# Adding the attention mask with VectorE as the scores leave PSUM, instead of with two TensorE products

## The chip, the cores and the metric

One NeuronCore of one Trainium2 chip runs the whole program; nothing is shared with another core. A NeuronCore has five engines with a queue each: TensorE (PE; matrix products into PSUM, with its weight loads shown apart as PEld), VectorE (DVE), ScalarE (ACT), GpSimd (POOL) and SyncE (SP), which here only issues DMAs. The metric is device microseconds of one execution, the median of several; lower is better.

## The reference, cut to what matters

Four sequences of 576 tokens go through masked attention with 8 heads of 64 columns, then through a gated layer (2304 tokens, 512 to 1536 to 512) and a soft mixture of 8 experts. The change concerns the attention:

```python
scores = scale * np.matmul(q, k.transpose(0, 1, 3, 2))
rel = pos[:, None] - pos[None, :]
mask_plain = (rel >= 0) & (rel < window)                                   # heads 0 to 3, window 32
mask_dil = (rel >= 0) & (rel < window * dilation) & (rel % dilation == 0)  # heads 4 to 7, dilation 4
scores = np.where(masks[None], scores, -1000000000.0)
scores = scores - np.max(scores, axis=-1, keepdims=True)
attn = np.exp(scores)
attn = attn / (np.sum(attn, axis=-1, keepdims=True) + 1e-09)
return np.matmul(attn, v)
```

A query sees at most 32 keys, which lie in a window of 64 keys for each group of 32 queries; the kernel computes the scores of these windows alone.

## The kernel before, in words

**Units.** The attention is cut into 20 units: five blocks of tokens (blocks 0 to 3 have 512 tokens, block 4 the 256 that remain) by four pairs of heads. A unit has the scores of two heads (`r`), each as a PSUM tile of 128 partitions by 4 x 64 columns, `s_ps[r]`, in the first half of a PSUM bank. `scores` (L140) fills it: first a product of a 128x128 identity with a mask tile (three masks of 256 columns in bf16, zero or a large negative number, in `msk`), which starts the accumulation (L148, once for each `r`), then 32 small products for each, 64 keys by 32 queries, that add the scores (L162). `softmax` (L172) takes on VectorE the maximum of each row and 64 columns, straight from PSUM (L176, once for each `r`), and subtracts it, from PSUM into the tile `s` in SBUF (L178, once for each `r`); then ScalarE takes the exponential in place (L184, 128x512), VectorE sums it (L186), adds 1e-9 (L187) and takes the reciprocal (L188), and VectorE (block 0) or GpSimd (later blocks) multiplies (L189). `turn_unit` transposes the result (L195, L196), `weighted` multiplies with v (L222), `finish_unit` splits the output into a high and a low part (L250 on ScalarE, L251 on VectorE) or copies it (L237, L238). From block 1 on, the output of the unit before the last is written into the second half of the same two banks (`beside["bank"]`), so two units share a bank: scores of the younger and output of the older one.

**Stages.** The head of the program (to about 28 us) works through the 4 units of block 0, with loads that were issued in a written order. Then layer 1 of block 0 runs on TensorE (`l1`, L455: 24 groups of 12 products 128x512, two groups for each of 12 column blocks), while 5 steps of later units and the conversion of the weights from a packed form (`convert`, L367: L379 on ScalarE, L380 and L381 on VectorE, L382 on GpSimd; split into high and low parts by `split_w`, L433 and L434) are placed between the groups. Layer 1 of block 1 follows with the rest of the units, to about 215 us; a `Spread` object decides after which group a step comes. After that: blocks 2 and 3 as a pair, block 4, the experts. Each group of layer 1 ends in a PSUM tile of a ring of two, which ScalarE's sigmoid (L477) or VectorE's multiplication (L479) empties.

**Order.** A planner places the instructions in the engines' queues when the program is built, by priorities and costs of its own; an engine works its queue in that order. Instructions marked by `keep_in_program_order` hold their written order among themselves: from layer 1 on, the score products, transposes and products with v are so marked (`at`, L137). Sigmoid and multiplication have a raised priority (L475). Waits are set by the framework; it lets two engines touch a PSUM bank only one after the other.

Of the kernel before, what the change touches and what calls it, by code (L numbers as in the profile page):

```python
# [13 lines left out]
ALU = mybir.AluOpType  # L14
AX = mybir.AxisListType
PSUM = bass.MemoryType.PSUM

P = 128
# [17 lines left out]
M_ID, M_COLS = 768, 896  # L36
# [9 lines left out]
def k_window(n, hp, t, i):  # L46
    if n < 4:
        return 32 * (4 * t + i) if hp < 2 else 160 * i + 32 * t
    return 160 * t + 32 * i if hp < 2 else 64 * (4 * t + i)
# [7 lines left out]
def tile_kernel(  # L57
# [10 lines left out]
    nc = tc.nc  # L68
# [17 lines left out]
    msk = cpool.tile([P, M_COLS], BF16, name="msk")  # L86
    cst = cpool.tile([P, C_COLS], F32, name="cst")
    mask = msk[:, 0:M_ID].rearrange("p (m c) -> p m c", m=3)
# [48 lines left out]
    def at(ins):  # L137
        return tc.keep_in_program_order(ins) if grouped[0] else ins

    def scores(u, ts):  # L140
        n, hp = u["id"]
        q, k = u["qk"][:, 0:512], u["qk"][:, 512:1536]
        if "s_ps" not in u:
            u["bank"] = [ps_a.tile([P, 512], F32, tag="a", name=f"s_ps{r}") for r in range(2)]
            u["s_ps"] = [x[:, 0:256].rearrange("p (t c) -> p t c", t=4) for x in u["bank"]]
            for r in range(2):
                at(
                    nc.tensor.matmul(  # L148
                        u["s_ps"][r].rearrange("p t c -> p (t c)"),
                        lhsT=msk[:, M_ID:M_COLS],  # L150
                        rhs=mask[:, 2 if n == 4 else (1 if hp >= 2 else 0)],
                        start=True,
                        stop=False,
                        skip_group_check=True,
                    )
                )
        for t in ts:
            for i in range(4):
                for r in range(2):
                    o = k_window(n, hp, t, i)  # L160
                    at(
                        nc.tensor.matmul(  # L162
                            u["s_ps"][r][32 * i : 32 * i + 32, t, :],
                            lhsT=q[64 * r : 64 * r + 64, 128 * t + 32 * i : 128 * t + 32 * i + 32],
                            rhs=k[64 * r : 64 * r + 64, o : o + 64],
                            start=False,
                            stop=True,
                            skip_group_check=True,
                        )
                    )  # L170

    def softmax(u, norm):  # L172
        s = u["s"].rearrange("p (a c) -> p a c", a=8)
        mx = sm.tile([P, 8], F32, tag="mx", name="mx")
        for r in range(2):
            nc.vector.tensor_reduce(mx[:, 4 * r : 4 * r + 4], u["s_ps"][r], AX.X, ALU.max)  # L176
        for r in range(2):
            nc.vector.tensor_tensor(  # L178
                s[:, 4 * r : 4 * r + 4],
                u["s_ps"][r],  # L180
                mx[:, 4 * r : 4 * r + 4].unsqueeze(2).to_broadcast([P, 4, 64]),
                ALU.subtract,
            )
        nc.scalar.activation(s, s, AF.Exp, scale=0.125)  # L184
        su = sm.tile([P, 8], F32, tag="su", name="su")
        nc.vector.tensor_reduce(su, s, AX.X, ALU.add)  # L186
        nc.vector.tensor_scalar(su, su, 1e-9, None, ALU.add)  # L187
        nc.vector.reciprocal(su, su)  # L188
        norm.tensor_tensor(s, s, su.unsqueeze(2).to_broadcast([P, 8, 64]), ALU.mult)  # L189
# [69 lines left out]
    def attn_steps(pbs, norm, head=None):  # L259
# [30 lines left out]
        def s_step(z, ts=range(4)):  # L290
            if z == 0 and 0 in ts:
                if head:
                    load_qk(0)
                    ld(nc.sync.dma_start(msk, masks.bitcast(BF16)))
                    load_qk(1)
                    ld(nc.sync.dma_start(cst, consts))
                    load_v(0)
                    load_qk(2)
                    load_v(1)
                    head()  # L300
                    load_qk(3)
                    load_v(2)
                    load_v(3)
                else:
                    first(load_qk)
                    first(load_v)
            scores(us[z], ts)
            if 3 not in ts:
                return
            if 2 <= z and not head:  # L310
                weighted(us[z - 2], range(2), us[z])
            softmax(us[z], norm)
            load(z + 2, load_qk)
            if z == 0:
                load(2, load_v)
# [703 lines left out]
    for f in range(NF):  # L1019
        c = f % 4  # L1020
# [18 lines left out]
    for e in range(8):  # L1039
        for h in range(2):  # L1040
            for kc in range(ND):
                nc.tensor.matmul(  # L1042
                    h_ps[h][32 * kc : 32 * kc + 32],
                    lhsT=st[:, kc, 32 * e : 32 * e + 32],
                    rhs=ew[0, e, h][:, kc],
                    start=(e == 0),
                    stop=(e == 7),
# [228 lines left out]
```

## Time and profile before

| | |
|---|---|
| time, median of 3 runs | 507.33 us (505.53 to 507.93) |
| span of the profiled execution, first to last instruction | 502.6 us (no other time of this execution is given) |
| instructions | 12872 |
| TensorE busy | 471.9 us, 94% of the span |
| VectorE busy | 312.1 us, 62% |
| ScalarE busy | 269.8 us, 54% |
| GpSimd busy | 158.1 us, 31% |
| DMA, largest queue | 111.06 MB, 59.2% of 16 engines |

The span is the profile's own time base: all positions below are microseconds from its start. An engine's busy share is a mean over stages that differ; the rows further down show stretches. In the profile's rows `L162` is line 162 of the kernel, "x64" a number of instructions, and a bracket `[0.58 <-ACT x_hi L250]` the time that the engine was idle before the row and what ended that idle time. A row with several instructions gives the time from the first start to the last end.

### The profile page before, as it was taken

How to read it: one execution, taken by the hardware profiler on the slowest of the kernel's cores; microseconds unless marked ns; L12 is line 12 of the kernel's file. 1: busy time of each engine (PE TensorE's matmuls, PEld its weight loads, DVE VectorE, ACT ScalarE, POOL GpSimd, SP SyncE). 2: the span in 40 equal slices, each digit the busy share in tenths (PEclk: the TensorE clock that was granted, in tenths of full speed). 3: DMA queues.
4: the chain of work that ended last, by engine and by line, in shares of the span. 5: the costliest groups of instructions: out<-in, count | busy, mean ns of one | idle time of the engine just before them, and what ended most of it. 6: DMA issues, size and time to landing. Idle time of an engine off the chain costs nothing.

```text
span 502.6 us, 12872 instructions
## 1 busy us (share of the span) xinstructions
PE 471.9 (94%) x5488; PEld 359.1 (71%) x5488; DVE 312.1 (62%) x629; ACT 269.8 (54%) x458; POOL 158.1 (31%) x132
## 2 busy tenths in 40 slices
PE   6889999899999998999789999999999999999993
PEld 3568877688787886786547888888888879842552
DVE  3978888748685755445967665665546765532632
ACT  2569657657697656544856455455436654300223
POOL 0244545415463514126045233333321124200100
PEclk9789999999999999999999999999999999999998
DMA  8979967985998059320002202202399986578997
GB/s 321 409 251 355 345 229 268 326 292 183 355 310 337 4 172 399 128 85 1 2 0 85 83 1 83 85 0 84 97 366 418 370 316 243 209 270 347 425 410 261
DMA packets 23786, 112.15 MB, mean 223 GB/s; under 512 B 2352, under 2 KB 7216, under 8 KB 14640
## 3 DMA queue, kind: packets, MB, share of 16 engines
q1 hardware_dynamic: 23408, 111.06, 59.2%
q8 instruction: 43, 0.70, 0.6%
q10 hardware_dynamic: 320, 0.26, 0.2%
q14 instruction: 15, 0.12, 0.1%
HBM read 97.16 MB, written 14.16 MB: 221 GB/s over the span
## 4 chain that ended last, share of the span: by engine, by line
PE 68%; DVE 6%; ACT 6%; DMA 2%; issue 2%; POOL 1%; SPq 0%; DVEq 0%; ACTq 0%; POOLq 0%
PE l1ps L467 23%; PE pa L589 11%; PE pe L589 6%; PE tp L754 4%; PE so_ps L1101 3%; PE lt_ps L718 3%; PE h_ps L1042 3%; PE pd L589 2%; PE s_ps L222 2%; PE sp L783 2%; DMA wo<-fw 2%; PE s_ps L162 2%; PE op L1140 1%; PE tr L195 1%; DVE s L553 1%
## 5 line engine op out<-in xcount | busy, mean ns | idle before, releaser
L467 PE MATMUL l1ps<-x_hi,whl 128*128 128x512 f32 x384 | 131.3, 407 | 5.7 <-ACT g L477 3.0
L467 PEld LDWEIGHTS l1ps<-x_hi,whl 128*128 128x128 f32 x384 | 72.2, 189 | 23.9 <-ACT g L477 4.2
L467 PE MATMUL l1ps<-x_lo,whl 128*128 128x512 f32 x192 | 76.3, 397 | 0.0
L382 POOL TENSOR_TENSOR fw<-fw 128x512 int32<-128x512 int32 x36 | 49.6, 1387 | 58.8 <-DVE fw L381 24.7
L479 DVE TENSOR_TENSOR g<-l1ps,g 128x512 f32<-128x512 f32 (+1 forms) x36 | 21.6, 599 | 32.4 <-PE l1ps L467 27.7
L467 PEld LDWEIGHTS l1ps<-x_lo,whl 128*128 128x128 f32 x192 | 36.6, 190 | 6.6 <-DVE x_lo L251 0.2
L467 PE MATMUL l1ps<-x,whl 128*128 128x256 f32 x288 | 37.3, 286 | 0.0
L467 PEld LDWEIGHTS l1ps<-x,whl 128*128 128x128 f32 x288 | 35.5, 192 | 0.6 <-ACT g L477 0.2
L434 POOL TENSOR_TENSOR whl<-w,whl 128x512 fp32r<-128x512 f32 x12 | 15.9, 1330 | 51.7 <-ACT whl L433 35.6
L477 ACT ACTIVATE g<-l1ps 128x512 f32<-128x512 f32 (+1 forms) x36 | 19.0, 527 | 22.4 <-PE l1ps L467 22.2
L754 PE MATMUL tp<-cst,g 128*128 128x128 f32 x216 | 27.9, 275 | 0.0
L754 PEld LDWEIGHTS tp<-cst,g 128*128 128x128 f32 x216 | 23.9, 140 | 5.1 <-issue 3.3
L759 ACT COPY gt<-tp 128x512 f32<-128x512 f32 x27 | 15.5, 583 | 21.2 <-PE tp L754 18.4
L379 ACT ACTIVATE fw<-st 128x512 f32<-128x512 f32 x36 | 22.7, 673 | 6.5 <-DMA st<-wd 6.3
L477 ACT ACT_TABLE_LOAD x20 | 25.7, 1283 | 0.4
L380 DVE TENSOR_SCALAR fw<-fw 128x512 uint32<-128x512 uint32 x36 | 23.5, 664 | 2.2 <-ACT fw L379 1.1
L434 POOL TENSOR_TENSOR whl<-wst,whl 128x512 fp32r<-128x512 f32 x12 | 16.3, 1357 | 25.1 <-ACT whl L433 17.9
L652 DVE TENSOR_TENSOR tm<-pe,tm 128x512 f32<-128x512 f32 x12 | 8.3, 690 | 23.7 <-PE pe L589 23.7
L176 DVE TENSOR_REDUCE mx<-s_ps 128x4 f32<-128x256 f32 x40 | 15.3, 414 | 11.1 <-PE s_ps L162 7.9
L189 POOL TENSOR_TENSOR sm<-sm,su 128x512 f32<-128x512 f32 x12 | 14.1, 1172 | 25.4 <-DVE su L188 25.4
L184 ACT ACT_TABLE_LOAD x16 | 20.5, 1283 | 1.0 <-PEq L1266 0.7
L434 DVE TENSOR_TENSOR whl<-fw,whl 128x512 fp32r<-128x512 f32 x24 | 19.1, 811 | 2.9 <-ACT whl L433 2.5
(462 smaller groups left out, 1006.9 us busy)
## 6 DMA issues: line engine op xcount, KB each, us to landing
ew<-w SPq DMA_DIRECT2D x32, 1024.0 KB, 8.7
st<-wd SPq DMA_DIRECT2D x18, 1024.0 KB, 9.1
wst<-wg SPq DMA_DIRECT2D x12, 1024.0 KB, 7.7
v<-qkv SPq DMA_DIRECT2D x20, 512.0 KB, 6.3
wg<-fw SPq DMA_DIRECT2D x12, 512.0 KB, 7.0
w<-wg SPq DMA_DIRECT2D x6, 1024.0 KB, 7.0
qk<-qkv SPq DMA_DIRECT2D x10, 576.0 KB, 6.0
qk<-qkv SPq DMA_DIRECT2D x8, 528.0 KB, 5.4
```

Source lines behind the costliest of these rows:

```text
L176: nc.vector.tensor_reduce(mx[:, 4 * r : 4 * r + 4], u["s_ps"][r], AX.X, ALU.max)
L184: nc.scalar.activation(s, s, AF.Exp, scale=0.125)
L379: nc.scalar.activation(top, st[:, c, 1].bitcast(F32), AF.Prelu, scale=2.0**-112, alpha=2.0**32)
L380: nc.vector.tensor_scalar(top.bitcast(U32), top.bitcast(U32), 3, None, ALU.logical_shift_left)
L382: nc.gpsimd.tensor_tensor(low.bitcast(I32), top.bitcast(I32), low.bitcast(I32), ALU.add)
L434: (nc.gpsimd if pool[h] else nc.vector).tensor_tensor(whl[:, 1, h], src[:, h], whl[:, 0, h].bitcast(F32), ALU.subtract)
L467: nc.tensor.matmul(pt[:, 0:nt], lhsT=whl[:, w_, a, dc, :], rhs=x_[n][:, dc, :], start=first, stop=(dc == HP_ORDER[-1] and w_ == 1),)
L477: nc.scalar.activation(g, pt[:, 0:nt], AF.Sigmoid)
L479: nc.vector.tensor_tensor(g, pt[:, 0:nt], g, ALU.mult)
L589: nc.tensor.matmul(pt, lhsT=w[:, w_, P * c : P * c + P], rhs=x_[:, c], start=first and c == 0 and w_ == 0 and x_ is hi, stop=c == 1 and w_ ...
L754: nc.tensor.transpose(tp[:, c], g_sb[self.n, 4 * q + c][:, P * j : P * j + P], ident)
L759: nc.scalar.copy(to, tp)
```

## The change

The two products of the identity and the mask go; the score products start their own accumulation. In `softmax` VectorE adds the mask to each of the two PSUM tiles and writes the sums into `s` in SBUF; the maximum and the subtraction then each take the whole 128x512 tile in SBUF in one instruction. The exponential and what follows stay.

```diff
@@ scores
-            for r in range(2):
-                at(
-                    nc.tensor.matmul(
-                        u["s_ps"][r].rearrange("p t c -> p (t c)"),
-                        lhsT=msk[:, M_ID:M_COLS],
-                        rhs=mask[:, 2 if n == 4 else (1 if hp >= 2 else 0)],
-                        start=True,
-                        stop=False,
-                        skip_group_check=True,
-                    )
-                )
...
-                            start=False,
+                            start=True,
                             stop=True,
@@ softmax
+        n, hp = u["id"]
+        m = mask[:, 2 if n == 4 else (1 if hp >= 2 else 0)].rearrange("p (t c) -> p t c", t=4)
         for r in range(2):
-            nc.vector.tensor_reduce(mx[:, 4 * r : 4 * r + 4], u["s_ps"][r], AX.X, ALU.max)
-        for r in range(2):
-            nc.vector.tensor_tensor(
-                s[:, 4 * r : 4 * r + 4],
-                u["s_ps"][r],
-                mx[:, 4 * r : 4 * r + 4].unsqueeze(2).to_broadcast([P, 4, 64]),
-                ALU.subtract,
-            )
+            nc.vector.tensor_tensor(s[:, 4 * r : 4 * r + 4], u["s_ps"][r], m, ALU.add)
+        nc.vector.tensor_reduce(mx, s, AX.X, ALU.max)
+        nc.vector.tensor_tensor(s, s, mx.unsqueeze(2).to_broadcast([P, 8, 64]), ALU.subtract)
         nc.scalar.activation(s, s, AF.Exp, scale=0.125)
```

## Rows read from the trace of the kernel before

**Rows 1.** Stretch; busy us (instructions) of PE, PEld, DVE, ACT, POOL; clock; DMA.

```profile
16.00:28.00 12.00, 10.18 (x211) 7.81 (x212) 11.23 (x24) 6.55 (x14) 4.31 (x3) 0.72 0.99 390
28.00:100.00 72.00, 67.28 (x898) 52.94 (x897) 58.79 (x116) 51.67 (x81) 34.00 (x27) 1.00 0.83 295
100.00:215.00 115.00, 112.35 (x1957) 89.12 (x1956) 70.91 (x156) 77.45 (x123) 45.06 (x36) 1.00 0.66 239
```

**Rows 2.** The same for L148 alone: PE and PEld busy, clock, DMA.

```profile
0.00:28.00 28.00, 1.80 (x8) 0.72 (x8) 0.82 0.94 362
28.00:100.00 72.00, 1.96 (x10) 0.58 (x10) 1.00 0.83 295
100.00:215.00 115.00, 4.29 (x22) 1.51 (x22) 1.00 0.66 239
```

**Rows 3.** TensorE's waits, 28 to 215 us: total, times, longest.

```profile
PE l1ps L467 <- ACT g L477: 3.0, 3, 1.7
...
```

**Rows 4.** Chain that ended last, in order of time: start, us, what.

```profile
100.72 0.23 PE s_ps L148 x2
```

**Rows 5.** Timeline of TensorE: start, us, instruction.

```profile
100.33 0.39 PE L467 MATMUL l1ps<-x_hi,whl 128*128 128x512 f32 x1
100.56 0.39 PE L148 MATMUL s_ps<-msk 128*128 128x256 bf16 x2
100.88 0.86 PE L162 MATMUL s_ps<-qk 64*32 64x64 f32 x64
```

**Rows 6.** VectorE's groups by form: busy us, mean ns | idle before.

```profile
L434 DVE TENSOR_TENSOR whl<-fw,whl 128x512 fp32r<-128x512 f32 x24 | 19.1, 811 | 2.9 <-ACT whl L433 2.5
...
L176 DVE TENSOR_REDUCE mx<-s_ps 128x4 f32<-128x256 f32 x40 | 15.3, 414 | 11.1 <-PE s_ps L162 7.9 <-PE s_ps L222 3.1
...
L178 DVE TENSOR_TENSOR sm<-s_ps,mx 128x256 f32<-128x256 f32 x32 | 11.9, 408 | 0.0
L186 DVE TENSOR_REDUCE su<-sm 128x8 f32<-128x512 f32 x16 | 10.9, 682 | 7.6 <-ACT sm L184 7.3
...
L189 DVE TENSOR_TENSOR sm<-sm,su 128x512 f32<-128x512 f32 x4 | 2.7, 680 | 0.0
```

**Rows 7.** Timeline of VectorE, 88.5 to 95.5 us.

```profile
89.54 0.74 DVE L176 TENSOR_REDUCE mx<-s_ps 128x4 f32<-128x256 f32 x2
90.21 0.74 DVE L178 TENSOR_TENSOR sm<-s_ps,mx 128x256 f32<-128x256 f32 x2
```

**Rows 8.** Timeline of ScalarE, the same stretch.

```profile
90.70 0.37 ACT L250 CAST x_hi<-s_ps 128x256 fp32r<-128x256 f32 x1 [3.16 <-DVE sm L178]
91.09 1.28 ACT L184 ACT_TABLE_LOAD   x1
92.39 0.63 ACT L184 ACTIVATE sm<-sm 128x512 f32<-128x512 f32 x1
...
94.33 0.60 ACT L477 ACTIVATE g<-l1ps 128x512 f32<-128x512 f32 x1
```

**Rows 9.** Timeline of ScalarE, 113 to 117 us.

```profile
113.50 1.28 ACT L184 ACT_TABLE_LOAD   x1
116.23 0.63 ACT L184 ACTIVATE sm<-sm 128x512 f32<-128x512 f32 x1 [1.45 <-DVE sm L178]
```

**Rows 10.** Timeline of GpSimd, 88.5 to 95.5 us.

```profile
89.70 1.29 POOL L382 TENSOR_TENSOR fw<-fw 128x512 int32<-128x512 int32 x1 [0.36 <-DVE fw L380]
```

**Rows 11.** Timeline of VectorE in the head.

```profile
12.33 0.42 DVE L176 TENSOR_REDUCE mx<-s_ps 128x4 f32<-128x256 f32 x1 [1.50 <-PE s_ps L162]
...
24.60 0.75 DVE L251 TENSOR_TENSOR x_lo<-xp,x_hi 128x256 fp32r<-128x256 f32 x2 [0.58 <-ACT x_hi L250]
```

**Rows 12.** Timeline of TensorE in the head.

```profile
11.13 1.18 PE L162 MATMUL s_ps<-qk 64*32 64x64 f32 x64 [2.44 <-DMA qk<-qkv]
```

**Rows 13.** The chain again, 181 to 192 us.

```profile
181.41 0.61 ACT g L477
...
182.35 8.59 DMA wo<-fw
```

## The prediction

> **What bounds the kernel now.** I read the busy time by stretch first. The 20 attention units run before 215 us, and the change touches nothing else. From 28 to 100 us TensorE is busy 67.28 of 72 us, from 100 to 215 us 112.35 of 115; VectorE has 58.79 and 70.91 there [rows 1]. So TensorE lacks 7.4 us in all, VectorE 57.3, of which only 13.2 lie ahead of 100 us. Before 28 us it is different: from 16 to 28 us VectorE is busy 11.23 of 12 us and TensorE 10.18, at a granted clock of 0.72. The removed products, looked up by their line, are 8 before 28 us, 10 up to 100 us and 22 after it [rows 2]: 4, 5 and 11 units. What TensorE waited for from 28 to 215 us is read next: the largest item is 3.0 us in three waits on ScalarE's sigmoid [rows 3]. The chain of waits runs through the products themselves: 0.23 us for the two of a unit [rows 4]. So 16 units stand in a stretch where TensorE sets the pace, and 4 in a head that DMA, VectorE and latency set.
>
> **TensorE: what goes.** Per unit two products 128x256 in bf16 leave. The chain gives the pair 0.23 us. From the start of the pair to the first score product 0.32 us pass (100.56 to 100.88), against 0.23 us from one layer-1 product to the next (100.33 to 100.56) [rows 5]; the 0.1 us by which 0.32 exceeds the chain's row may be what the switch to the small score products costs, and then it stays. I take 0.23, with 0.32 as the upper end and, as lower end, nothing where TensorE would have to wait anyway. 16 units x 0.23 = 3.7 us (0 to 5.1). The other score products only get another start flag: same count, same shape, nothing.
>
> **VectorE: what comes.** Before, a unit has two maxima 128x256 from PSUM (414 ns) and two subtractions 128x256 from PSUM (408): 1.64 us. After, two additions, one maximum and one subtraction over 128x512 in SBUF. The addition is not in the trace; nearest is the subtraction from the same PSUM tile, 408 ns; its second operand is a bf16 tile in SBUF, and I take the same figure (ends: 0.34, half of what 128x512 in SBUF took, and 0.49, 408 by the ratio of 811 to 680 below). The maximum has a twin, the sum over 128x512 in SBUF, 682 ns. The subtraction has a twin in the head's normalisation, 128x512 with a broadcast operand, all in SBUF, 680 ns; the low parts of the weights, also two SBUF operands, took 811 ns on average [rows 6]. Sum 0.82 + 0.68 + 0.68 = 2.18 us, so +0.54 us per unit (+0.4 to +0.8 by these ends). From 100 us on, 11 x 0.54 = 5.9 us lie in 44 us of idle VectorE; from 28 to 100 us, 5 x 0.54 = 2.7 us in 13.2. I cost both at nothing; with the cover gone they cost 5.9 and 2.7, at the upper end 8.8 and 4.0.
>
> **The path to the sigmoid.** What matters more than VectorE's sum is what ScalarE waits for. At 89.54 us VectorE starts the maxima, at 90.21 the subtractions [rows 7]. ScalarE, idle 3.16 us until the first subtraction is over, then evacuates the older unit's output from the same bank (90.70), loads a table (91.09), takes the exponential (92.39), and after another load the sigmoid (94.33) [rows 8], which TensorE awaits (the 1.7 us of rows 3). So the bank holds the evacuation, and that holds table load and exponential: 2.85 us from the first maximum to the exponential. The load does not itself wait for the scores: at 113.50 one ran, and the exponential then stood idle 1.45 us for the subtraction [rows 9]. After the change the first bank is read once. The evacuation may start after one addition (0.41 us), and with it and the load (0.37 + 1.28) the exponential could start some 2.1 us after the first addition; VectorE's 1.41 us (89.54 to 90.95) become about 1.95. So the exponential comes some 0.7 us earlier where this order holds, in two of the three waits. Up to -1.3 us; below, nothing, or +0.54 at each of three where the evacuation is planned behind the exponential (+1.6). I take -0.6: one of the two.
>
> One term stands against it. The maxima and subtractions kept their 0.74 us a pair while GpSimd ran an addition in SBUF from 89.70 to 90.99 [rows 7, 10], and their large operand lies in PSUM. The new subtraction has both operands in SBUF, like the weights' low parts, whose mean is 131 ns above the 680 of the head [rows 6]. GpSimd is busy 79 of the 187 us [rows 1], so a subtraction meets it in 42% of cases and may be held for up to one such addition (1.29 us). Worked out as half of it at 42%, that is 0.27 us a unit; it stays inside VectorE's idle time, except in the rival below.
>
> [...]
>
> **The head.** Units 0 and 1 get +1.1 us of VectorE time, but VectorE then stands idle 1.50 us until the scores of unit 2, which wait 2.44 us for their q and k from HBM [rows 11, 12]; hidden. The first scores no longer stand behind the mask's transfer and products (0.3 us at most): hidden by the same transfer. The 0.54 us of unit 2 lie ahead of the first weight conversion in VectorE's queue, and so of the first block's layer 1; those of unit 3 ahead of a spot where VectorE is idle 0.58 us [rows 11]. I take +0.5 us, one unit's; ends 0 and +2.4 (two units, each subtraction held 0.65). Eight products fewer also leave TensorE idle a little longer in a stretch at clock 0.82 [rows 2]; scores took 1.18 us after the idle stretch at 11.13 us [rows 12], and 0.86 in the other units, so up to 0.3 us for each of two units; I take nothing.
>
> **Sum.** -3.7 - 0.6 + 0.5 = -3.8 us on a span of 502.6. After 215 us everything hangs on TensorE's order and moves along. The span is 4.7 us under the median of 507.33 (the page gives no other time of that execution); I keep this distance: 503.5 us. The likeliest case alone: 501.5 to 506.
>
> **Rivals.**
> *VectorE becomes the bound before 100 us (slower).* It is 94% busy from 16 to 28 us and 82% from 28 to 100 [rows 1]; a conversion chain (VectorE, GpSimd, ScalarE, VectorE) feeds layer 1 there. If the 7 units from unit 2 on put their whole increase on the path, with the hold at GpSimd, that is 7 x (0.54 + 0.27 to 0.65) = 5.7 to 8.3 us, less the 3.7 from TensorE: +2.0 to +4.6, some 510.5. It decides from the point where the increase exceeds VectorE's idle time between two layer-1 groups that need a converted weight. Against it: 13.2 us idle for 5 units. For it: rows 3 show waits on the sigmoid that end in a busy VectorE.
> *The gain is given back (same).* The chain goes through a transfer of 8.59 us at 182.35, which starts after the sigmoid of 181.41 [rows 13]. Were it bound to the DMA queue and not to that sigmoid, the 14 units ahead of it would win nothing (14 x 0.23 = 3.2 us); with the head's 0.5 us, 507. A planner that orders the engines' queues anew from its own costs can also take 2 to 3 us: the waits of rows 3 are that large.
> *More is gained.* The pair is worth 0.32, and both waits on the sigmoid shrink: -5.1 - 1.3 + 0.5 = -5.9, 501.5.
> That the products stay cannot be: nothing else writes the mask.
>
> **Chances.** Forecast 0.45, more gained 0.13, given back 0.23, VectorE bound 0.19. A change of 0.5% (2.5 us, under 504.8 or over 509.9) is about what a measurement can tell. Of the forecast's 0.45 some 0.32 lies under 504.8; with 0.13 of the larger gain, 0.45 faster. The rest of the forecast (0.13), the given-back case (0.2) and a small part of the VectorE case (0.04) make 0.37 the same; 0.18 slower. Range 500.5 to 510: it reaches into the slower case, and leaves out its far end and that of the large gain.
>
> **What would show it.** No product of the mask's line; layer-1 product to first score product in 0.23 to 0.33 us; TensorE's busy time from 28 to 215 us down by about 3.7 us, and the stretch shorter by as much. Additions at 0.41 us, the maximum at 0.68, the subtraction at 0.68 alone and near 1.3 where GpSimd runs. ScalarE's evacuation starting behind the first addition. Wrong if TensorE's waits on the sigmoid grow from 3.0 us beyond 6, if the first full run of layer 1 starts over 1.5 us later, or if the transfer near 182 us does not move.

## The result: 1.2% slower, and the profile after

The changed kernel takes 512.12 us (median of 4 runs, 510.76 to 514.06); the kernel before, run on the same chip, took 506.43 (4 runs, 505.01 to 507.93). The ratio is 1.0124, 95% interval 1.0077 to 1.0170. Forecast were 503.5 us and a range to 510. Ratios leave out runs over 1.5% above the fastest of their kernel (six of those tabled below), medians hold all. The profiled execution took 510.76 us with a span of 509.0, at a mean granted clock of 0.976 (before: a span of 502.6 us, 0.986).

The stretches of the changed kernel, columns as in [rows 1]:

```profile
16.00:28.00 12.00, 10.92 (x224) 8.48 (x224) 10.87 (x27) 6.25 (x14) 3.07 (x3) 0.68 0.96 375
28.00:100.00 72.00, 67.24 (x885) 52.61 (x886) 62.61 (x115) 50.47 (x80) 32.39 (x25) 0.98 0.82 290
100.00:215.00 115.00, 107.40 (x1851) 85.42 (x1850) 75.60 (x158) 77.33 (x119) 48.29 (x36) 0.97 0.67 243
```

From 100 to 215 us TensorE is busy 5 us less than before, but there is not less time: it is idle instead, and its clock, 1.00 before, is 0.97. Where the 6.4 us of span went is seen best by when TensorE reaches the same work (start of the product named, from the timelines of TensorE):

| | before | after | after minus before |
|---|---|---|---|
| unit 3, first score product | 17.26 | 19.73 | +2.5 |
| unit 5, first score product | 40.06 | 43.20 | +3.1 |
| unit 7 | 70.22 | 73.36 | +3.1 |
| unit 9 | 100.88 | 100.89 | 0.0 |
| unit 17 | 174.25 | 173.50 | -0.7 |
| layer 1, group 39 (the 40th) | 190.67 | 189.95 | -0.7 |
| group 41 | 203.06 | 206.04 | +3.0 |
| group 43 | 210.29 | 216.03 | +5.7 |
| group 47 | 228.63 | 234.35 | +5.7 |

So there are three parts: 3.1 us lost in the head, 3.9 us gained from 70 to 190 us (the size that was forecast, but not by the forecast's terms, as the experiments e1 and e2 below show), and 6.4 us lost between 190 and 216 us. The last 0.7 us of the span come behind 229 us and are not followed here. This "offset" is used below for every run.

**VectorE's new instructions**, by form (busy us, mean ns):

```profile
L420 DVE TENSOR_TENSOR whl<-fw,whl 128x512 fp32r<-128x512 f32 x24 | 22.1, 926 | 4.5 <-ACT whl L419 3.8
...
L167 DVE TENSOR_TENSOR sm<-s_ps,msk 128x256 f32<-128x256 f32 x32 | 12.2, 415 | 11.3 <-PE s_ps L151 9.3 <-PE s_ps L208 2.0
L169 DVE TENSOR_TENSOR sm<-sm,mx 128x512 f32<-128x512 f32 x16 | 12.2, 760 | 0.1
L168 DVE TENSOR_REDUCE mx<-sm 128x8 f32<-128x512 f32 x16 | 10.8, 677 | 0.1
...
L169 DVE TENSOR_TENSOR qk<-qk,mx 128x512 f32<-128x512 f32 x4 | 2.7, 680 | 0.0
```

The addition takes 415 ns and the maximum 677, as estimated. The subtraction takes 680 in four units and 760 on average in the 16 others. The weights' low parts, 811 ns before [rows 6], now take 926.

**The head.** VectorE before, then after (both in order of time):

```profile
9.29 1.46 DVE L186 TENSOR_REDUCE su<-sm 128x8 f32<-128x512 f32 x2
...
15.49 0.43 DVE L380 TENSOR_SCALAR fw<-fw 128x512 uint32<-128x512 uint32 x1 [0.33 <-ACT fw L379]
...
16.68 1.33 DVE L380 TENSOR_SCALAR fw<-fw 128x512 uint32<-128x512 uint32 x1
```

```profile
12.68 0.42 DVE L167 TENSOR_TENSOR sm<-s_ps,msk 128x256 f32<-128x256 f32 x1 [1.68 <-PE s_ps L151]
13.02 1.27 DVE L172 TENSOR_REDUCE su<-sm 128x8 f32<-128x512 f32 x2
...
17.21 0.42 DVE L366 TENSOR_SCALAR fw<-fw 128x512 uint32<-128x512 uint32 x1
...
19.60 0.41 DVE L367 TENSOR_SCALAR fw<-st 128x512 int32<-128x512 uint32 x1
```

Before, VectorE summed units 0 and 1 and then stood idle until unit 2's scores came [rows 11]. After, the planner has put unit 2's first addition ahead of these sums: VectorE is idle with the sums ready behind it. They run at 13.02, not at 9.29, and everything behind them is late, the normalised weights of unit 0 (TensorE's longest wait of the head) and the conversion of the first packed weight, `fw`, on which layer 1 and the next loads hang. That wait, in the changed kernel:

```profile
PE tr L181 <- DVE sm L175: 2.9, 1, 2.9
```

And SyncE's store of the first converted weight, before and after:

```profile
19.39 0.33 SPq L365 DMA_DIRECT2D wg<-fw  x1
```

```profile
21.86 0.33 SPq L351 DMA_DIRECT2D wg<-fw  x1
```

All engines' busy time, and TensorE's clock (the last number but two), from 8 to 40 us, before and after:

```profile
8.00:40.00 32.00, 25.67 (x516) 18.03 (x514) 25.84 (x61) 17.91 (x32) 8.66 (x6) 0.84 0.89 343
```

```profile
8.00:40.00 32.00, 22.01 (x496) 15.45 (x495) 26.35 (x56) 14.76 (x28) 8.65 (x6) 0.80 0.82 318
```

**The late place.** The chain of waits of the changed kernel, which answers to [rows 13]:

```profile
179.21 0.45 PE tr L181 x4
...
179.73 0.33 SPq L255
...
181.05 9.61 DMA wo<-fw
...
190.76 0.76 DVE fw L367 x2
191.52 0.60 DVE su L172
...
193.00 1.04 POOL qk L175
194.04 0.37 POOL fw L368
...
195.40 1.74 POOL fw L368
197.14 1.23 POOL whl L420
...
198.41 0.50 PE l1ps L453
```

The transfer `wo<-fw` is the store of an earlier converted weight; its end frees the buffer into which VectorE (L367) converts the next. It was issued 1.3 us earlier than before, as forecast, but took 9.61 us, not 8.59, and ended at 190.66, not 190.94. TensorE's lead is lost there. Then 198.41 against 197.52 before: 7.75 us from landing to product against 6.58. The reason is again the order on VectorE. The sum of unit 18 (`su`, L172 above) now stands behind the two L367 that wait for the buffer; before, it stood ahead of them:

```profile
189.79 0.69 DVE L186 TENSOR_REDUCE su<-qk 128x8 f32<-128x512 f32 x1 [1.52 <-ACT qk L184]
191.03 0.76 DVE L381 TENSOR_SCALAR fw<-st 128x512 int32<-128x512 uint32 x2 [0.55 <-DMA wo<-fw]
```

So GpSimd's multiplication starts at 193.00 (192.54 before), and its two additions take 3.15 us, not 2.67, beside VectorE's low part. TensorE's waits at this place, a timeline of the changed kernel:

```profile
195.50 0.66 PE L394 MATMUL wt_ps<-cst,fw 128*128 128x128 f32 x4 [2.17 <-POOL fw L368]
198.41 0.50 PE L453 MATMUL l1ps<-x_hi,whl 128*128 128x512 f32 x1 [1.33 <-POOL whl L420]
```

Before, it waited 1.00 and 0.35 us. A third gap of 1.07 us, until 201.82 us, has no releaser in the profile. And then its clock falls. The same two stretches, before and after:

```profile
200.00:204.00 4.00, 4.00 (x46) 2.92 (x40) 2.17 (x7) 2.09 (x3) 0.00 (x0) 1.00 1.02 359
204.00:208.00 4.00, 4.00 (x50) 3.13 (x49) 2.54 (x8) 3.06 (x9) 1.93 (x2) 1.00 0.36 148
```

```profile
200.00:204.00 4.00, 2.93 (x60) 2.60 (x55) 1.64 (x4) 0.91 (x3) 0.04 (x1) 0.63 1.00 341
204.00:208.00 4.00, 4.00 (x16) 2.89 (x18) 0.89 (x2) 0.95 (x3) 0.00 (x0) 0.51 0.23 94
```

From 201.05 to 207.9 us the granted clock is 0.50. Layer-1 products follow each other every 0.43 us there (next row, of the chain), not every 0.23 [rows 5]:

```profile
203.26 3.84 PE l1ps L453 x9
```

### The profile page after: what moved, and what is told of

Same layout as the page of the kernel before. It is cut to its first block, busy times and chain, and to the rows that moved or that the text cites. A ratio compares the mean times of both kernels' runs of the same rounds, so it can differ in the third digit from the quotient of the medians.

```text
span 509.0 us, 12802 instructions
## 1 busy us (share of the span) xinstructions
PE 471.5 (93%) x5448; PEld 359.1 (71%) x5448; DVE 321.0 (63%) x629; ACT 270.7 (53%) x458; POOL 159.4 (31%) x132
## 4 chain that ended last, share of the span: by engine, by line
PE 65%; DVE 8%; ACT 4%; DMA 3%; issue 2%; POOL 2%; SPq 0%; DVEq 0%; ACTq 0%; POOLq 0%
PE l1ps L453 21%; PE pa L575 11%; PE pe L575 6%; PE tp L740 3%; PE lt_ps L704 3%; PE h_ps L1028 3%; PE so_ps L1087 2%; PE pd L575 2%; PE s_ps L208 2%; DMA wo<-fw 2%; PE sp L769 2%; PE s_ps L151 2%; PE tr L181 1%; PE wt_ps L394 1%; PE op L1126 1%
## 5 line engine op out<-in xcount | busy, mean ns | idle before, releaser
L453 PE MATMUL l1ps<-x_hi,whl 128*128 128x512 f32 x384 | 133.5, 411 | 4.9 <-ACT x_hi L236 2.7
L453 PEld LDWEIGHTS l1ps<-x_hi,whl 128*128 128x128 f32 x384 | 73.4, 192 | 23.4 <-ACT x_hi L236 3.2
L368 POOL TENSOR_TENSOR fw<-fw 128x512 int32<-128x512 int32 x36 | 50.7, 1415 | 54.8 <-DVE fw L367 20.4
L463 ACT ACTIVATE g<-l1ps 128x512 f32<-128x512 f32 (+1 forms) x36 | 19.0, 527 | 24.4 <-PE l1ps L453 24.2
L420 DVE TENSOR_TENSOR whl<-fw,whl 128x512 fp32r<-128x512 f32 x24 | 22.1, 926 | 4.5 <-ACT whl L419 3.8
L419 ACT CAST whl<-fw 128x512 fp32r<-128x512 f32 x24 | 14.8, 619 | 18.6 <-POOL fw L368 16.7
L420 POOL TENSOR_TENSOR whl<-wst,whl 128x512 fp32r<-128x512 f32 x12 | 16.2, 1352 | 26.4 <-DVE su L174 11.8
L367 DVE TENSOR_SCALAR fw<-st 128x512 int32<-128x512 uint32 x36 | 18.8, 549 | 5.6 <-DMA st<-wd 2.6
L366 DVE TENSOR_SCALAR fw<-fw 128x512 uint32<-128x512 uint32 x36 | 20.9, 592 | 1.6 <-ACT fw L365 1.3
```

What stands on the lines that cost most here:

```text
L366: nc.vector.tensor_scalar(top.bitcast(U32), top.bitcast(U32), 3, None, ALU.logical_shift_left)
L367: nc.vector.tensor_scalar(low.bitcast(I32), st[:, c, 0], 2.0**-29, None, ALU.mult)
L368: nc.gpsimd.tensor_tensor(low.bitcast(I32), top.bitcast(I32), low.bitcast(I32), ALU.add)
L420: (nc.gpsimd if pool[h] else nc.vector).tensor_tensor(whl[:, 1, h], src[:, h], whl[:, 0, h].bitcast(F32), ALU.subtract)
L453: nc.tensor.matmul(pt[:, 0:nt], lhsT=whl[:, w_, a, dc, :], rhs=x_[n][:, dc, :], start=first, stop=(dc == HP_ORDER[-1] and w_ == 1),)
L463: nc.scalar.activation(g, pt[:, 0:nt], AF.Sigmoid)
```

## The experiments

Ratios are against the kernel before in the same session (median 505.9 to 507.3 us; 123 runs of it in all, 503.2 to 510.8). "Clock shortfall" is span x (1 - mean granted clock), averaged over all runs of a kernel. In the text, "old form" is that of the kernel before (mask products on TensorE; maximum and subtraction from PSUM), "new form" that of the changed one.

| kernel | us, median (runs) | ratio, 95% | shortfall, us |
|---|---|---|---|
| before, all sessions | 506.6 (123) | | 7.1 |
| changed | 512.12 (4) | 1.0077 to 1.0170 | 16.3 |
| e1 new form, products back but dead | 511.35 (10) | 1.0041 to 1.0113 | 12.6 |
| e2 products gone, old form | 510.53 (10) | 0.9996 to 1.0077 | 12.3 |
| e5 idle products at the late place | 509.82 (10) | 1.0033 to 1.0093 | 12.5 |
| e6 late weight products a step later | 511.56 (4) | 1.0029 to 1.0176 | 17.1 |
| e3 head old | 508.39 (10) | 0.9996 to 1.0074 | 11.7 |
| e7 idle products in the head | 517.65 (4) | 1.0146 to 1.0290 | 16.2 |
| e8 idle products in both places | 514.30 (4) | 1.0103 to 1.0228 | 10.9 |
| e9 the same in the kernel before | 510.47 (4) | 1.0041 to 1.0191 | 8.3 |
| e10 head's order held | 511.17 (8) | 1.0058 to 1.0129 | 18.6 |
| e15 the same, products dead | 510.24 (8) | 1.0035 to 1.0093 | 16.3 |
| e11 unit 18 old | 509.05 (12) | 1.0014 to 1.0074 | 15.4 |
| e12 head and unit 18 old | 506.86 (12) | 0.9971 to 1.0026 | 10.2 |
| e14 before, unit 18 new | 509.33 (12) | 1.0007 to 1.0074 | 9.1 |
| e16 e12 with two transfers earlier | 504.21 (12) | 0.9922 to 0.9975 | 9.2 |
| e17 before with them | 504.28 (12) | 0.9919 to 0.9978 | 6.5 |
| e18 changed with them | 506.44 (12) | 0.9958 to 1.0012 | 14.4 |
| e19 e18, units 0 and 1 old | 508.96 (12) | 1.0031 to 1.0081 | 15.7 |
| e20 e18, units 2 and 3 old | 505.74 (12) | 0.9953 to 1.0012 | 14.6 |

An offset is read from one profiled execution of a kernel. In the head e3, e12, e14, e16 and e17 have the order of the kernel before on VectorE, ScalarE and GpSimd, and their offsets at 40 us are -0.8 to +1.3; e5, e6, e11 and e18 have that of the changed kernel, and theirs are +2.0 to +4.5 (the changed kernel: +3.1). So the two orders stand apart, but a single offset scatters by some 2 us.

**Each half of the change alone.** The first theories: VectorE's new form is to blame (B), TensorE's missing products are (C), or both, through waits and clock (A).

```
# e1: the changed kernel, plus the mask products, overwritten by the scores
+   nc.tensor.matmul(s_ps[r], lhsT=identity, rhs=mask, start=True, stop=True)
...
# e2: the kernel before, without them (so without the mask)
-   nc.tensor.matmul(s_ps[r], lhsT=identity, rhs=mask, start=True, stop=False)
```

> The changed kernel with the two mask products of each unit back on TensorE, but dead: they start and end a group of their own in the score bank, and the score products overwrite it; VectorE still adds the mask. So TensorE's work is that of before, VectorE's that of after. Theory A (the loss is made at one place, near 195 to 202 us, where TensorE waits for the last weight conversion, and its clock then falls to half for 6.8 us): TensorE comes 3.7 us later to that place, waits there less, the clock holds; 509 us against 506.4 before and 512.1 after. Theory B (VectorE's 0.54 us a unit is the bound of the head and of layer 1 up to 100 us, as in my slower rival): nothing is won back and 3.7 us are added, 515 to 516 us. Theory C (the products mattered as activity of TensorE, everywhere): 506 to 507 us.

> The kernel before without the mask products and without any mask (left out of the computation): two maxima and two subtractions from PSUM on VectorE, as before. TensorE's work is that of after, VectorE's that of before. Theory A: 503 us if the clock holds at the last conversion, 506 to 508 if TensorE, 3.7 us earlier there, waits so long that the clock falls. Theory B: 502.7 us, the whole of TensorE's 3.7 us. Theory C: 508 us or more, with more half-clock time in the records.

The first loses 0.8%: 511.35 us lie between A (509) and B (515 or more), and far from C. The second loses 0.4%, with an interval that just reaches 1: 510.53 us and more shortfall, where C had it, and A had not. No one theory holds for both, and neither half is to blame alone. At 40 us the offset is +2.6 with VectorE's form alone and +1.0 with the products gone alone (within the scatter of unchanged heads), against +3.1 for the change.

The two runs also tell where the gain from 70 to 190 us comes from. The changed kernel gains 3.9 us there; e1, with all products back on TensorE, gains 3.8; e2, without them, loses 0.7. TensorE's waits on the sigmoid between 28 and 215 us, 3.0 us before [rows 3], are gone in the changed kernel and in e1, and have grown in e2:

```profile
PE l1ps L456 <- ACT g L466: 5.1, 6, 2.8
```

So the gain belongs to VectorE's new form, not to the products taken off TensorE. How the waits went is seen on ScalarE, here in the changed kernel at the place of [rows 8]:

```profile
92.92 0.70 ACT L236 CAST x_hi<-s_ps 128x256 fp32r<-128x256 f32 x2 [0.59 <-DVE sm L167]
93.52 0.61 ACT L463 ACTIVATE g<-l1ps 128x512 f32<-128x512 f32 x1
94.14 1.28 ACT L170 ACT_TABLE_LOAD   x1
95.94 0.63 ACT L170 ACTIVATE sm<-sm 128x512 f32<-128x512 f32 x1 [0.52 <-DVE sm L169]
```

The sigmoid (L463) now runs ahead of the exponential and its table load; before, it stood behind them and a load of its own. So it is near 79 us too, and in e1; e2 has the order of before. The gain, like the losses below, goes with a changed order of a queue; no run held this order apart from the rest of the new form. The removed products show little: from 100.9 to 190 us TensorE is busy 2.0 us less than before, but idle 1.3 us more, and 0.7 us are left.

**The late place, filled or moved.**

```
# e5: in the changed kernel, ahead of the sum (L409 of the changed kernel) of the fifth output weight
+   for _ in range(8): nc.tensor.matmul(wide[:, 0:256], lhsT=pt[:, 0], rhs=cst[:, 0:256], ...)
...
# e6: the steps of the last weight one step later
-   slot_weights(2 * y, fw, 3)
+   slot_weights(2 * y, fw, 4 if y == 5 else 3)
```

> The changed kernel with eight idle products 128x256 in f32 on TensorE in the places near 193 to 202 us where it waits for the last weight conversion (they read the small tile that VectorE has just copied, and write a PSUM bank that the next product overwrites). Nothing else moves by more than a few places in a queue. Theory A: the clock stays at full level from 196 to 216 us, and the 3.4 us of half-clock work there go; 508 to 509 us against 512.1. Theory B: no gain, 512 to 513 us. Theory C: as A or better, but then e1 must be near 506.

> The changed kernel with the four steps on the last converted weight (transposes, product, sum) one layer-1 group later (lag 4 instead of 3 for the last piece), so that TensorE does not reach the first transposes before the conversion is done. Theory A: the 2.2 us wait near 195 us goes and with it the half-clock stretch; 506 to 507 us, perhaps 505. Theory B: 512 us. A middle case: the wait moves to the layer-1 weight split that GpSimd makes at 197 us (1.3 us), the clock falls all the same; 510 us.

With idle products in the gap the clock is 1.00 from 196 to 208 us, here from 200 us on, where it was 0.63 and 0.51 without them:

```profile
200.00:204.00 4.00, 4.00 (x23) 3.52 (x24) 2.57 (x7) 2.10 (x4) 0.48 (x1) 1.00 1.02 340
204.00:208.00 4.00, 4.00 (x26) 2.87 (x25) 1.49 (x4) 3.29 (x5) 1.04 (x1) 1.00 0.40 167
```

The place loses 4.0 us, not 6.4. The times are 509.82 against 512.12 us, though the intervals of the two ratios overlap. In e6 TensorE waits 3.9 us at once for the low part `whl` and the clock falls as in the changed kernel (layer-1 products 0.43 us apart from 204.85 to 207.41 us); only the middle case came true. By these traces holding the clock is worth some 2.4 us there, and the longer waits (3.50 us, 1.35 before) and the gap of 1.07 us make up most of the rest.

**The head.**

```
# e3: the changed kernel, block 0 (n == 0) in the old form
+   if n == 0: <mask products; maximum and difference from PSUM>
...
# e7, e8, e9: idle float32 products 128x256 in the head
+   if head and z == 2: fill(us[z]["qk"], 5)
...
+   if 1 in ts: fill(pt_ring[:, z % 4], 2)
```

> The four units of the head (both layers' first batch row, 8 products) keep the old form, mask by TensorE and maximum and difference out of PSUM; the 16 others are as after the change. If the clock is what is lost (theory A: the time is the work and waits at full clock, some 494 us, plus half of the time at half clock, 16 after the change against 7 before), the half-clock time of the head returns to that of before, the offset at 37 us falls from +3.2 to within 0.5 us, and the time is 508 to 509.5: the stretch near 200 us still loses. If VectorE's longer work in the head is what costs (theory B), the same 3 us are gained, but the granted clock from 8 to 28 us stays as after the change. If the loss sits near 200 us alone, 511 to 512.

> The changed kernel, with idle float32 products 128x256 in the head whose results nothing reads: five behind the scores of unit 2, two behind each unit's weighted sum of v. VectorE's work stays that of the changed kernel. Theory A: half-clock time in the head falls by some 3 to 6 us, and with it the time by 1.5 to 3: 509 to 510.5. Theory B (VectorE's work sets the head): no gain, 511.5 to 513, since the idle products only add to TensorE.

> The changed kernel with the idle products of the head and the eight idle ones ahead of the late stretch near 197 us. Theory A: half-clock time as before the change or less (7 us lost or less), work and waits near 495: 504 to 506.5, faster than the kernel before. Theory B: as with the late idle products alone, 509 to 511.

> Control: the kernel before the change with the same idle products in both places. If the idle products help by holding the clock where the change let it fall, they win little here: 505.5 to 508. If they help any kernel alike, as much as they help the changed one (5 us or more): 502 or less.

With the head old the offset at 40 us is -0.7, and the time 508.39 us, as A and B both had it: the head's loss is the change's in these four units. The granted clock of the head rose with it, as A had it: 0.95 from 8 to 40 us, against 0.80 in the changed kernel and 0.84 in the one before. But e1 and e2, in this order, have

```profile
8.00:40.00 32.00, 22.07 (x502) 15.48 (x502) 26.21 (x56) 15.17 (x29) 8.30 (x6) 0.89 0.83 313
```

```profile
8.00:40.00 32.00, 24.97 (x502) 17.78 (x502) 25.17 (x61) 16.05 (x31) 8.23 (x6) 0.79 0.89 330
```

At 0.89 e1 has lost 2.6 us by 40 us, at 0.79 e2 has lost 1.0; and e3, well above the kernel before in clock, is only 0.7 us ahead of it. So the clock does not decide the head's loss. Of the idle products nothing came: 14 instructions in a row at 20 to 25 us stood in TensorE's queue ahead of the second unit's transposes, and the first layer-1 product came at 32.0 us (19.0 before). They cost the kernel before 4 us too (e9). As a test of the clock the three runs fail; they show that idle products at these places in the head do harm.

**Order in VectorE's queue.**

```
# e10: sums of units 0 and 1 into columns that unit 2's additions will write
+   raw = sm4[:, 2].rearrange("p (a c) -> p a c", a=8)[:, :, hp // 2]
...
# e11: unit 18 alone old; e12: block 0 and unit 18 old; e14: before, unit 18 alone new
+   if (n, hp) == (4, 1): <old form>
```

> The changed kernel in all 20 units, with one order held in the head: the sums of units 0 and 1 are first written into the columns that unit 2's additions will write, so VectorE can't take these additions ahead of the sums, as it did after the change (there they waited 1.68 us for scores, and the sums behind them). VectorE's work is unchanged. If that order is what the head loses by, TensorE's 2.88 us wait for the first normalised weights (16.08 us) falls below 1.3, the offset at 40 us falls from +3.1 to within 1 us, and the time is 508 to 509.5. If VectorE's longer instructions are what costs, nothing of it changes: 511 to 513.

> The changed kernel with unit 18 alone in the old form. In the changed kernel VectorE takes unit 18's sum behind two instructions that wait for the packed weight from HBM (landing 190.7); with this unit old the sum stands ahead of them again. VectorE is idle 2.6 us there, so the 0.54 us of this unit can't matter by themselves. If the order is the cause of the late loss, GpSimd's multiplication starts 0.4 us or more earlier after the landing, and the offset from 190 to 216 us grows by less than 2 us instead of 6.5: 507 to 509. If lost TensorE work (lead and clock) alone is the cause, one unit of 20 changes nothing: 511 to 512.5.

> The changed kernel with the four units of the head and unit 18 in the old form, the other 15 changed: both places in the order of before. If the two orders are the whole loss, what is left is the gain of 15 units: 502.5 to 505, faster than the kernel before. If the half clock near 200 us comes from the lost lead whatever the order, 508 as with the head alone.

> The kernel before with unit 18 alone in the new form: the order at the late place flips (its sum behind the two instructions that wait for the weight), all else stays. If that order is the cause of the late loss, the time rises by 2 to 5 us over the kernel before: 508.5 to 511. If not, it stays within 1 us of it: 506 to 507.5.

The late place is shown from both sides. (What the first expectation calls the packed weight from HBM is the store of `wo` described above, which holds the buffer.) One unit of 20 put back (e11) takes the loss between 190 and 216 us from 6.4 to 2.7 us (under 2 was expected), and the time to 509.05; one unit made new in the kernel before (e14) costs it 0.4%, 2.7 us by the medians, 1.9 of them at this place in its trace. In e11 the sum stands ahead of the pair again, in e14 behind it. VectorE stands idle for 2.6 us ahead of the pair, so the 0.54 us of a unit don't matter by themselves; that leaves its sum's place (the unit's two products came and went with it). e12 missed: it stands 4.2 us ahead at 190 us, but 0.5 at 216. The chain gives the reason: its store is issued 4.8 us earlier than before and lands only 2.9 earlier (row of its chain),

```profile
177.59 10.46 DMA wo<-fw
```

and TensorE waits 2.22 and 1.34 us (1.00 and 0.35 before), at a clock of 0.83 and 0.75 in the two stretches from 192 to 200 us.

e10 took away TensorE's 2.9 us wait (0.6 us now), but not the head's loss (+3.4 at 40 us): held like this, other work moved, and the first converted weight was stored at 21.71 us, no earlier than in the changed kernel. It leaves the question open.

**The queue at the late place, and the head once more.** In SyncE's queue of the kernel before a load of q and k waits for its buffer, and three transfers stand behind it:

```profile
180.48 0.33 SPq L269 DMA_DIRECT2D qk<-qkv  x1
180.86 0.96 SPq L276 DMA_DIRECT2D v<-qkv  x1
181.87 0.44 SPq L361 DMA_DIRECT2D st<-wd  x1
182.35 0.43 SPq L365 DMA_DIRECT2D wo<-fw  x1
```

From 170 to 180 us the DMA engines have next to nothing to do (shares of 0.00 and 0.01), and e18 below could issue the same store at 159.8. e16 to e18 put the store and the load of the last packed weight ahead of it; e15 is e10 with the dead products.

```
    def beside():
+       store()
+       if n_conv[0] == len(turn) - 2:
+           stage(turn[-1])
        sab()
```

> The changed kernel with the order of the head's sums held, as in the run before on the head's order, and the two mask products of each unit back on TensorE, dead (the scores overwrite them). If the head loses by the order of VectorE's queue and by TensorE's clock together, and not by VectorE's longer instructions, the offset at 40 us falls from +3.1 (changed), +2.6 (dead products without the order) and +3.4 (order without the products) to within 1 us: 508.5 to 510. If VectorE's longer work is the cause, it stays at +2.5 or more: 511 to 512.5.

> The mixed kernel (four units of the head and unit 18 old, 15 new), and SyncE's queue holds the store of the fourth converted output weight, and the load of the last packed one, ahead of the load that waits from 160 to 176 us for its buffer, not behind it. If that queue gives back the mixed kernel's gain of 4 us, the offset stays at -3 or less behind 215 us: 502 to 504.5, faster than the kernel before. If something else gives it back (the clock, or the loads behind them), 506 to 507.5.

> Control: the kernel before with the same two transfers ahead in SyncE's queue. TensorE waited 1.4 us for the converted weight there and 1.1 at issue, so at most 2.5 us are to be had: 504 to 506.5. If it gains as much as the mixed kernel, the transfers are a gain of their own and have given nothing back.

> The changed kernel with the same two transfers ahead: the wait of VectorE's queue for the buffer at 188 to 191 us goes, and with it the late order's harm and the late loss, while the head's +3.1 stays, to be won back by 101 us as before. If the late loss is this wait alone, 505 to 507.5. If it is TensorE's fewer products alone, 510.5 to 512.5.

In e18 the same transfers are issued at

```profile
159.80 0.33 SPq L351 DMA_DIRECT2D wo<-fw  x1
160.29 0.33 SPq L347 DMA_DIRECT2D st<-wd  x1
160.67 0.71 SPq L255 DMA_DIRECT2D qk<-qkv  x1
```

and TensorE's stretch from 190 to 216 us, first in the changed kernel, then in e18, is

```profile
190.00:216.00 26.00, 20.89 (x242) 15.92 (x240) 12.56 (x27) 13.01 (x24) 9.78 (x7) 0.87 0.57 214
```

```profile
190.00:216.00 26.00, 23.62 (x327) 18.73 (x327) 13.14 (x27) 14.52 (x27) 6.12 (x6) 1.00 0.49 173
```

The late loss is gone, all of it (offset -0.4 at 190 us and -0.4 at 210), and the fall of the clock with it: 506.44, 5.7 us under the changed kernel. The kernel before gains 2.5 us by the same step (e17), so some 3 us of the change's loss were this queue's (3.2 by the medians, 4.4 by the ratios); the 2.2 us by which e18 still stands over e17 are left for the head (e18: +3.3 at 40 us). e16 and e17, at 504.2 and 504.3, beat the kernel before and the changed one, and between them 15 units of the change make no difference.

e16 kept its time but not its offset, which was to stay at -3 or less behind 215 us: it is -4.0 at 190 us and -0.4 at 210. TensorE stood still for 3.5 us in the products with v, without a releaser in the profile, and ran at 0.72 and 0.50 in the two stretches from 192 to 200 us:

```profile
195.77 0.42 PE L231 MATMUL s_ps<-pt_ring,v 64*64 64x16 f32 x9 [3.49 <-issue]
```

And e16 gains no more over e12 (2.6 us) than e17 over the kernel before (2.5). By the expectation of e17 that means that the two transfers are a gain of their own, and that the lead of 4 us that this mix of old and new units (e12, e16) has at 190 us is lost to something else, which stays open.

e15 missed, and shows why e10 had: the weight conversion came later still, its store at 27.63 us and the next packed load with it at 26.21 (16.67 before), so the offset at 40 us was +4.9. A last pair asked about the head's order without holding anything:

```
# e19: e18 with units 0 and 1 old        # e20: e18 with units 2 and 3 old
+   if n == 0 and hp in (0, 2): <old form>
...
+   if n == 0 and hp in (1, 3): <old form>
```

> The changed kernel with the two transfers ahead in SyncE's queue, and units 0 and 1 in the old form. VectorE's sums of units 0 and 1 then stand ahead of unit 2's addition, as before the change. If this order is what the head loses by, TensorE's wait for the first normalised weights is under 1.5 us (2.9 in the changed kernel), the offset at 40 us is +1 or less (+3.3 with the transfers alone), and the time is 503.5 to 505. If it is the products that TensorE lost and its clock, half of the head's loss stays, as with units 2 and 3 old: +1.5 to +2.5, 505 to 506.

> The same with units 2 and 3 old in place of 0 and 1: as many products back, as much less VectorE work, but unit 2's first maximum, which waits for scores, stands ahead of the sums of units 0 and 1, as in the changed kernel. If the order is what the head loses by, the offset at 40 us stays at +2.3 or more, and the time at 506 to 507. If it is the products and the clock, +1.5 to +2.5 and 505 to 506, like the other run.

The wrong way round: with the sums ahead of unit 2's addition (e19) 508.96 and +4.6 at 40 us, with them behind (e20) 505.74 and +1.7. Whether these sums stand ahead of that addition does not decide by itself. What the runs agree on is the conversion of the first weight, of which the sums are only one of the things in front: in e19 its second half stood behind the low parts of unit 0's output. Over the 16 profiled kernels without idle products in the head and without e15, the 8 that issue the store of that weight before 21 us (19.25 to 20.37) have a mean offset at 40 us of +0.1, the 8 that issue it after (21.34 to 22.25) of +3.3; the correlation is 0.85. That is a correlation, not a test: other things moved too, and the 16 have only seven orders of the head between them (six share that of the kernel before, five that of the changed one).

## Why the prediction was wrong

**TensorE's term (-3.7).** This step, the largest term of the sum, failed: "16 units x 0.23 = 3.7 us" are hardly to be found. With the products gone and VectorE's old form (e2) TensorE is 0.9 us slower than before from 40 to 190 us; with the products back and the new form (e1) it is 3.9 us faster, as much as in the changed kernel. The prediction's lower end, nothing, is nearer: time that TensorE no longer worked became time in which it stood idle.

**The path to the sigmoid (-0.6, at most -1.3).** Mis-sized, and by another mechanism. The three waits, 3.0 us, are gone altogether. ScalarE does evacuate behind the first addition, as worked out (0.59 us idle at 92.92 us). But the exponential does not come earlier in front of the sigmoid; the sigmoid goes first. That both terms together made -4.3 and the offset fell by 3.9 is luck: one was too large, the other too small.

**The distance of 4.7 us between span and median.** In every run on record the time exceeds the span by 1.7 to 1.9 us only; so the profiled execution before was a fast one, of some 504.4 us (an estimate), and the 4.7 us were no constant of the kernel. The miss of 8.6 us does not come from there: the median of four runs, 506.43 us, is 0.9 us below the one used.

**The head (+0.5, ends 0 and +2.4).** The term that was mis-sized: it measures +3.1, beyond its end. I named the right victim ("The 0.54 us of unit 2 lie ahead of the first weight conversion in VectorE's queue") and took VectorE's queue to keep its order. The new order has 1.27 us of sums behind a wait of 1.68 us as well. TensorE was idle longer from 8 to 40 us (10.0 us against 6.3) and its clock lower (0.80 against 0.84), but e1 and e2 show that this does not decide. That the order alone does it was tried and not shown (e10, e19); that these four units do it was (e3), and e1 and e2 point to VectorE's new form rather than to the missing products.

**"After 215 us everything hangs on TensorE's order and moves along".** This step failed most. The rival of the gain given back stood in the prediction, with the transfer at 182.35 us; I took it to move with the sigmoid of 181.41. Its issue did move, by 1.3 us, its end by 0.3: it is the last of four in SyncE's queue, at a DMA share of 1.01 from 184 to 192 us. And I let the rival cost no more than the gain. It cost 6.4 us, since the sum of unit 18 slipped behind the pair that waits for this store (e11, e14), and the clock fell behind the wait (0.50 from 201.05 to 207.9 us; 1.00 there with the wait filled, e5). With the queue changed it costs nothing (e18).

**"Eight products fewer also leave TensorE idle a little longer ...: I take nothing".** The clock carries a part of the loss, and not mainly in the head. Shortfall grows from 7.1 to 16.3 us, and each half of the change alone raises it by 5 us (e1, e2). Within one kernel, over the 162 runs of the 18 experiments that enter the ratios, a run with 1 us more shortfall is 0.57 us longer (correlation 0.72). By that the 9.2 us would be worth 5.2, an estimate, and the measured difference is 5.7. But this is a correlation: at the late place a wait lengthened the run and the clock fell to 0.50 behind it, so the two come together, and e18, with 7.3 us more shortfall than the kernel before, takes no longer. What a run shows of the clock by itself is the 2.4 us of the late place (e5).

Theory A, as the expectation of e3 words it, has a run pay the whole shortfall. Here a run pays 0.57 of it on average; that part of the slow stretches lies where TensorE waits anyway would explain it, but no run shows that apart.

**VectorE as the bound before 100 us.** The rival's mark, layer 1 starting more than 1.5 us later, came true (18.98 to 20.84), its sum did not: from 40 to 100 us nothing more is lost, and the 3.1 us by which VectorE is busier there (53.4 against 50.2 us) stay hidden. GpSimd's hold on the subtraction is 80 ns on the mean (760 against 680), below the 131 that I had from the row. Of the 16 subtractions ten ran without GpSimd beside them, in 0.64 to 0.69 us; three began while GpSimd was in an addition or subtraction of its own, and took 1.07 to 1.12; three had begun 0.16 us before one, and took 0.68, while GpSimd's addition took 1.67 us and not 1.29. So in these six meetings the one that started later took longer. Over all 16 that comes to less than the prediction's 0.27 us a unit, since only three were the later one, and each of them for the last 0.5 to 0.6 us of GpSimd's instruction. The low parts, whose mean rose from 811 to 926 ns, meet GpSimd too: one with GpSimd idle took 0.68 us (at 64.47), one that began during GpSimd's additions 1.43 (at 194.56).

**Open.** What in the head decides between +0.1 and +3.3 us, beyond the conversion's place in VectorE's queue; whether ScalarE's order alone makes the gain before 190 us; and what takes the lead of e12 and e16 behind 190 us.

## What to carry to other kernels

Where a planner or scheduler orders in-order queues, a changed duration is also a changed order: for each wait on a transfer, ask which ready instruction may now stand behind it, and in which queue. Before crediting work taken from the bound engine, look for the waits and the next transfer that do not move with it; the gain ends there, and the idle time in front of it can cost the clock too (0.50 here behind 3.5 us of waits and a gap of 1.07; 1.00 with the wait filled, e5). And test each half of a change alone, even where the sum seems to come out: here the half that was to gain gained nothing (e2). A dependent store that sits in a queue behind a load that waits for a buffer was worth more here (2.5 us, e17) than taking 40 products off TensorE.

## What was not expected of the hardware

A few microseconds of waiting were followed by a granted clock of 0.50: TensorE had waited 3.5 us in two pieces (until 195.5 and 198.4 us of the changed kernel) and 1.1 more (until 201.8), and from 201.05 to 207.9 us the granted clock was 0.50, though TensorE was busy for 6.08 of these 6.85 us. Eight idle products, 16 instructions some 0.22 us apart in the trace, kept it at 1.00 in the same place (e5).

A stream of small products with v stalls now and then without a releaser in the profile ("issue"): 3 times, 3.4 us in all from 28 to 225 us of the changed kernel, twice and 1.2 us before, once for 3.5 us in e16. No run here tried it apart.
